# Hash attention and a two-layer block on one core: loads of three batches issued by GpSimd, and two copies moved within the second product

## The chip, the core and the metric

The kernel runs on one core of a Trainium2 chip. The core has a matrix engine (TensorE, PE), a vector engine (VectorE, DVE), an activation engine (ScalarE, ACT), a general engine (GpSimd, POOL) and a queue processor (SyncE, SP). SP, ACT and POOL can each issue DMA transfers; all of them are carried out by the core's 16 DMA engines. The metric is the device time of one execution in microseconds (us), as the median of several runs.

## The reference

```
q_bits = (q @ proj > 0); k_bits = (k @ proj > 0)          # 6 bits a row
mask   = bucket(q_bits) == bucket(k_bits)
attn   = softmax(where(mask, q @ k.T / 8, -1e9))          # rows
x      = (attn @ v) laid out as [batch, seq, heads*64]
out    = x + relu(layernorm(x) * g_ln @ w_ch1) @ w_ch2
```

There are 4 batches of 8 heads, 768 rows and 64 columns a head; the block's width is 512 and its hidden width 2048. All inputs and outputs are float32.

## The kernel before

**Chunks and rounds.** The output is made in 12 chunks of 256 rows, three to a batch. The loop over `n` (lines 867 to 882) is called a round here. In round n the kernel weaves together four things by program order: the attention of chunk n (scores L435, exponentials L445 on ACT, products with the values L469, division L489 to L497 on DVE), the norm of chunk n-1 (L516 to L518 and the transposing DMA L538 that makes `xnT`), the first product of the block for chunk n-1 ("up", L566, eight parts `u`), and the second product for chunk n-2 ("down", L607, eight parts `d`, four for each half of the chunk's rows). The last part of each half is followed by L612 on DVE, which adds the result to `x`, and by L616 on SP, which writes `x` out. The order is written out by hand in the strings of `steps`: `n` is the norm, `d` and `u` are parts of the products, and a capital with two digits is a step of the preparation of a batch and a half (four heads): `N30` is step N for batch 3, half 0. `interleave` (L681) lays these strings between the pieces of the attention by their costs.

**Preparation of a batch.** It runs a few rounds ahead, in halves. `L` loads queries and keys (`load_half`, L138), `W` loads values (`load_values`, L157). `N` makes bf16 copies on POOL (L282), `T` transposes them into `slots` by DMA (L304, then a move L309), `B` transposes 32 by 32 blocks on DVE (L287), `H` takes the hash products on PE (L318), turns them into bits on DVE (L326, L329), writes the bits to memory (L331) and reads them back in four pieces into `slots` (L333). `V` makes bf16 values and their sums on POOL (L344 to L353). `E` ("share") is one matmul of those sums on PE (L358) and a copy of its result by DVE into `vsum` (L359). `Q` squares queries and keys in place on ACT (L180), only for a check of their size; it is spread over the pairs of attention pieces by `singly`, and the load that stands beside it there follows its last step, after the eighth of a round's twelve pieces.

**Buffers.** `qnat` and `knat` have four buffers, so the load of batch b, half h, takes the buffers of batch b-2, half h, and waits until their squares are done. `vnat` has one buffer: `W` waits for the cast L344 of the values before it. The PSUM pool `ps_mm` has two banks, which the halves of the second product, the parts of the first, the hashes and the shares take by turns. A tile takes the bank that was given back first in program order. `xnT` has one buffer.

**Queues.** Each engine works its own instructions off strictly in program order, and a DMA-issuing instruction that waits holds up everything behind it on that engine. Before the change SP issues the loads of batches 2 and 3 in four pieces for each half (two heads each of q and k), the value loads of batch 1 half 1 and of batches 2 and 3, all transposing DMAs, the hash bits' eight small moves of each batch, and all outputs but the last two small ones. POOL issues the weights and the loads of batch 1 but its second value half.

The string of round 5, for instance, is

```python
5: "n d d d E20 V21 d d d d d u u u W30 u u E21 u u u",
```

and the loads beside the squares are

```python
singly = {
    2: "Q00 L20", 3: "Q01 L21", 4: "Q10 L30", 5: "Q11 L31",
    6: "Q20", 7: "Q21", 8: "Q30", 9: "Q31",
}
```

Of the kernel before, what the change touches and what calls it, by code (L numbers as in the profile page):

```python
# [30 lines left out]
def kernel(  # L31
# [11 lines left out]
    nc = tc.nc  # L43
# [83 lines left out]
    def load_half(b, half):  # L127

        h0 = half * H // 2
        t = {}  # L130
        for nm in "qk":
            t[nm] = nat.tile([P, H // 2, NC, D], F32, tag=f"{nm}nat", name=f"{nm}nat")

        cuts = [[0, 1, 2, 4] if half == 0 else [0, 2, 4], [0, 4], [0, 2, 4], [0, 2, 4]][b]
        for lo, hi in zip(cuts, cuts[1:]):
            for nm, src in (("q", q), ("k", k)):
                eng = nc.gpsimd if b == 1 else nc.scalar if nm == "k" and hi - lo == 1 else nc.sync
                eng.dma_start(  # L138
                    out=t[nm][:, lo:hi],
                    in_=src[b, h0 + lo : h0 + hi].rearrange("h (p c) d -> p h c d", p=P),  # L140
                )
        if b == 0 and half == 0:
            nc.scalar.activation(wake2[:, 0:1], wake2[:, 1:2], AF.Exp)
            t["v"] = load_values(b, half)
        return t

    def load_values(b, half):
        h0 = half * H // 2
        eng = nc.gpsimd if (b, half) == (1, 0) else nc.sync
        if (b, half) == (0, 1):  # L150

            t = work.tile([P, NH * CT // 2], F32, tag="h", bufs=1, name="vnat1")[
                :, 0 : H // 2 * NC * D
            ].rearrange("p (h c d) -> p h c d", h=H // 2, c=NC)
        else:
            t = nat.tile([P, H // 2, NC, D], F32, tag="vnat", bufs=1, name="vnat")
        eng.dma_start(  # L157
            out=t, in_=v[b, h0 : h0 + H // 2].rearrange("h (p c) d -> p h c d", p=P)
        )
        return t  # L160

    class Prep:
# [7 lines left out]
        def load(self, half):  # L170
            self.tiles.setdefault(half, {}).update(load_half(self.b, half))

        def load_v(self, half):
            self.tiles.setdefault(half, {})["v"] = load_values(self.b, half)
# [561 lines left out]
    def first_two():  # L736
# [77 lines left out]

    steps = {
# [8 lines left out]
    }  # L824
    plain = "n d d d d d d d d u u u u u u u u"
# [249 lines left out]
```

## Time and profile before

| what | value |
|---|---|
| time, median of 3 runs | 325.58 us (323.94 to 326.59) |
| time of the profiled execution | 322.48 us, of which its span is 319.8 us |
| mean granted clock of PE in it | 0.991 |
| loads issued by POOL, q and k of batch 1 | 768 KB each; median from issue to landing 14.4 us (q), 15.7 us (k) |
| the one value load issued by POOL | 17.4 us to landing |
| `xnT` transposing DMA (L538) | 10 of them, median 3.1 us to landing |
| queue q1 (issued by SP and ACT: L138, L304, L309, L331, L333, L538, L616 and others) | 31.59 MB |
| queue q0 (issued by POOL) | 8.13 MB |

The span is the time from the first instruction to the last in one profiled execution; 2.7 us of that execution's time lie outside it. "Busy" counts an engine's instructions. An idle stretch is put down to what came last before the next instruction could start; an idle stretch of an engine that is not the bottleneck costs nothing. The time to landing counts from the issue, so it holds what stood before the transfer in its queue.

### The profile page before, as it was taken

The page shows a single profiled execution, that of the slowest core. Times are in us where ns is not written, and L with a number is a line of the kernel's source. Part 1 is how long each engine was busy: PE and PEld are TensorE (multiplying, and loading weights), DVE is VectorE, ACT ScalarE, POOL GpSimd, SP SyncE. Part 2 cuts the span into 40 slices and gives each one's busy share as a digit, 9 for nine tenths or more (in the row PEclk, how much of TensorE's full clock was granted, in tenths as well). Part 3 has the DMA queues.
Part 4 walks back from the last instruction along what each step waited for, and adds up shares of the span by engine and source line. Part 5 has one row for each costly group of instructions (what it writes and reads, how often), then busy time and mean ns, then how long its engine had stood idle before and what let it go on. Part 6 is the DMA issues. An engine that isn't in the chain of part 4 may idle for free.

```text
span 319.8 us, 7815 instructions
## 1 busy us (share of the span) xinstructions
PE 304.4 (95%) x3245; PEld 228.8 (72%) x3268; DVE 187.5 (59%) x404; ACT 215.9 (68%) x272; POOL 84.8 (27%) x110
## 2 busy tenths in 40 slices
PE   7879999999999999979999999999999999999993
PEld 6556787688579669648768758769779678687563
DVE  1799996374873865723666677545643734735421
ACT  4686977776668767657777767788779667565020
POOL 3467530901900181132091091010100100100200
PEclk9999999999999999998999999999999999999998
DMA  7999997379486696492564464120030120200302
GB/s 227 363 200 301 210 340 113 66 143 255 140 166 193 162 159 148 120 338 65 183 141 103 123 143 103 29 69 34 2 87 14 28 73 1 68 35 0 101 0 76
DMA packets 64970, 40.94 MB, mean 128 GB/s; under 512 B 47152, under 2 KB 59952, under 8 KB 64928
## 3 DMA queue, kind: packets, MB, share of 16 engines
q1 hardware_dynamic: 60224, 31.59, 38.6%
q0 software_dynamic: 4128, 8.13, 10.9%
q10 hardware_dynamic: 576, 0.66, 0.6%
q8 instruction: 27, 0.44, 0.6%
q14 instruction: 15, 0.12, 0.1%
HBM read 27.98 MB, written 6.88 MB: 109 GB/s over the span
## 4 chain that ended last, share of the span: by engine, by line
PE 81%; DVE 9%; DMA 6%; issue 1%; ACT 1%; POOL 0%; SPq 0%; DVEq 0%; POOLq 0%
PE hp L566 27%; PE o L607 20%; PE sc L435 17%; PE av L469 10%; DMA xnT<-xn 5%; PE hash L318 3%; DVE slots L238 3%; DVE slots L262 2%; PE tpose L200 1%; PE o L589 1%; DMA knat<-in_k_dram 1%; DVE xn L518 1%; DVE stats L516 1%; DVE x L497 1%; PE hash L252 1%
## 5 line engine op out<-in xcount | busy, mean ns | idle before, releaser
L445 ACT ACTIVATE ex<-sc,expb 128x1024 bf16<-128x1024 f32 x144 | 159.4, 1112 | 65.7 <-PE sc L435 63.3
L566 PE MATMUL hp<-xnT,w_sb 128*128 128x256 bf16 x768 | 99.7, 274 | 3.5 <-DMA xnT<-xn 3.2
L607 PE MATMUL o<-w_sb,hbuf 128*128 128x512 bf16 x345 | 90.7, 379 | 1.8 <-DVE x L612 0.9
L435 PE MATMUL sc<-slots 70*128 70x256 bf16 x576 | 87.1, 273 | 2.3 <-POOL slots L238 1.6
L566 PEld LDWEIGHTS <-w_sb 128*128 128x128 bf16 x768 | 72.3, 98 | 13.4 <-DMA xnT<-xn 4.0
L469 PEld LDWEIGHTS <-ex 128*128 128x128 bf16 x1152 | 54.5, 98 | 15.1 <-ACT ex L445 1.3
L435 PEld LDWEIGHTS <-slots 70*128 70x128 bf16 x576 | 51.8, 97 | 18.2 <-issue 4.9
L576 DVE TENSOR_SCALAR hbuf<-hp 128x512 bf16<-128x512 f32 x48 | 32.9, 686 | 46.4 <-PE hp L566 46.3
L469 PE MATMUL av<-vaug,ex 128*128 128x65 bf16 x1152 | 59.0, 194 | 0.3 <-ACT ex L445 0.2
L529 POOL TENSOR_SCALAR rs<-mv 128x2 f32<-128x2 f32 x12 | 8.6, 713 | 168.9 <-DVE mv L517 168.8
L607 PEld LDWEIGHTS <-hbuf 128*128 128x128 bf16 x368 | 33.8, 97 | 26.9 <-issue 1.2
L612 DVE SCALAR_TENSOR_TENSOR x<-o,rs,x 128x512 f32<-128x512 f32 x23 | 17.3, 751 | 41.0 <-PE o L607 36.1
L578 ACT ACTIVATE hbuf<-hp 128x512 bf16<-128x512 f32 x48 | 28.5, 594 | 18.8 <-PE hp L566 18.8
L497 DVE TENSOR_TENSOR x<-x,rc 128x256 f32<-128x256 f32 x36 | 18.2, 506 | 1.2
L518 DVE SCALAR_TENSOR_TENSOR xn<-x,mv,gbc 128x512 bf16<-128x512 f32 x24 | 18.1, 759 | 0.8
L344 POOL CAST vaug<-vnat 128x1536 bf16<-128x1536 f32 x8 | 12.2, 1527 | 21.2 <-DMA vnat<-in_v_dram 21.2
L516 DVE BATCH_NORM_STATS2 stats<-x 128x6 f32<-128x512 f32 x24 | 16.5, 691 | 0.4
L490 DVE TENSOR_TENSOR x<-av,vsum 128x256 f32<-128x256 f32 x36 | 14.9, 414 | 0.0
L489 DVE TENSOR_SCALAR rc<-av 128x4 f32<-128x4 f32 x36 | 5.6, 157 | 13.5 <-PE av L469 13.5
L180 ACT ACTIVATE qnat<-qnat 128x768 f32<-128x768 f32 x16 | 13.3, 833 | 0.0
L180 ACT ACTIVATE knat<-knat 128x768 f32<-128x768 f32 x16 | 13.3, 833 | 0.0
L353 POOL TENSOR_TENSOR vsum<-vsum,vaug 128x256 f32<-128x256 f32 x18 | 12.5, 697 | 1.4
(86 smaller groups left out, 218.2 us busy)
## 6 DMA issues: line engine op xcount, KB each, us to landing
out_dram<-x SPq DMA_DIRECT2D x23, 256.0 KB, 4.3
vnat<-in_v_dram SPq DMA_DIRECT2D x7, 768.0 KB
qnat<-in_q_dram SPq DMA_DIRECT2D x11, 384.0 KB, 4.3
knat<-in_k_dram SPq DMA_DIRECT2D x11, 384.0 KB, 6.7
w_sb<-in_moe_w_ch_dram POOLq DMA_DIRECT2D x4, 1024.0 KB, 14.0
slots<-slots SPq DMA_DIRECT2D x6, 384.0 KB, 4.9
qnat<-in_q_dram POOLq DMA_DIRECT2D x2, 768.0 KB, 14.4
knat<-in_k_dram POOLq DMA_DIRECT2D x2, 768.0 KB, 15.7
```

Of the source, the lines that this page charges most:

```text
L180: nc.scalar.activation(src, src, AF.Square, accum_out=sq[:, a, col : col + 1],)
L435: nc.tensor.matmul(sc[:, i, :], key_block(h, kj), query_blocks(h),)
L445: nc.scalar.activation(ex, sc, AF.Exp, bias=expb[:, 1:2] if b else expb[:, 0:1], scale=scale if b else scale / Q_SCALE,)
L469: nc.tensor.matmul(av[:, h - ha, qi, :], state[g][:, i, qi * P : (qi + 1) * P], va[:, h, kj, :], start=(b > 0 and (g, i, qi) == (0, 0, 0)) ...
L497: nc.vector.tensor_tensor(xv, num, rc.unsqueeze(3).to_broadcast([P, 2, TT, D]), op=AOP.mult)
L516: nc.vector.bn_stats(stats, x[:, i, :])
L518: nc.vector.scalar_tensor_tensor(xn[:, :, i, :], x[:, i, :].rearrange("p (o d) -> p o d", d=P), mv[:, i, 0:1], gbc.rearrange("p (o d) -> p ...
L566: nc.tensor.matmul(hp[:, i, :], w1_sb[:, dt, nt * P : (nt + 1) * P], st["xnT"][:, dt, :], start=(dt == 0), stop=(dt == ND - 1),)
L576: nc.vector.tensor_scalar_max(dst, src, 0.0)
L578: nc.scalar.activation(dst, src, AF.Relu)
L607: nc.tensor.matmul(o2, st["h"][:, nt, i * P : (i + 1) * P], w2_sb[:, nt, :], start=(nt == 0), stop=(nt == NH - 1),)
L612: nc.vector.scalar_tensor_tensor(x[:, i, :], o2, st["rs"][:, i : i + 1], x[:, i, :], op0=AOP.mult, op1=AOP.add,)
```

## The change

Two things are changed. First, every load of queries, keys and values of batches 1 to 3 is now issued by POOL, and the queries and keys of a half come in one transfer of four heads each in place of two of two heads. In all 21 issues leave SP (16 of 384 KB and 5 of 768 KB) and 13 of 768 KB are added on POOL, at the same places of the program. Second, in `steps` the shares E11, E20, E30 and E31 stand two or three parts of the second product later, after its sixth part; V21 moves with E20.

```diff
-        cuts = [[0, 1, 2, 4] if half == 0 else [0, 2, 4], [0, 4], [0, 2, 4], [0, 2, 4]][b]
+        cuts = ([0, 1, 2, 4] if half == 0 else [0, 2, 4]) if b == 0 else [0, 4]
         for lo, hi in zip(cuts, cuts[1:]):
             for nm, src in (("q", q), ("k", k)):
-                eng = nc.gpsimd if b == 1 else nc.scalar if nm == "k" and hi - lo == 1 else nc.sync
+                eng = nc.gpsimd if b else nc.scalar if nm == "k" and hi - lo == 1 else nc.sync
...
     def load_values(b, half):
         h0 = half * H // 2
-        eng = nc.gpsimd if (b, half) == (1, 0) else nc.sync
+        eng = nc.gpsimd if b else nc.sync
...
-        3: "n d d d N20 d N20 B20 E11 d T20 d B20 W20 d d B20 u B20 u H20 u u u u u u",
+        3: "n d d d N20 d N20 B20 d T20 d E11 B20 W20 d d B20 u B20 u H20 u u u u u u",
...
-        5: "n d d d E20 V21 d d d d d u u u W30 u u E21 u u u",
+        5: "n d d d d d d E20 V21 d d u u u W30 u u E21 u u u",
...
-        7: "n d d d N31 d N31 B31 E30 d T31 d B31 d d B31 u B31 V31 u H31 u u u u u u",
-        8: "n d d d E31 d d d d d u u u u u u u u",
+        7: "n d d d N31 d N31 B31 d T31 d E30 B31 d d B31 u B31 V31 u H31 u u u u u u",
+        8: "n d d d d d d E31 d d u u u u u u u u",
```

On PE the order is otherwise the same but for one pair: in round 8 a group of scores and a part of the second product change places. On DVE the copies L359 of E20 and E31 move behind the L612 of the first half and the next division; those of E11 and E30 keep their place. On SP nothing changes but that the loads are gone.

## The prediction

> **What bounds the kernel now.** I read the page's shares by engine first, then the slices, then the windows and timelines around the slice that stands out.
>
> ```profile
> PE 304.4 (95%) x3245; PEld 228.8 (72%) x3268; DVE 187.5 (59%) x404; ACT 215.9 (68%) x272; POOL 84.8 (27%) x110
> PE   7879999999999999979999999999999999999993
> PEclk9999999999999999998999999999999999999998
> PE 81%; DVE 9%; DMA 6%; issue 1%; ACT 1%; POOL 0%; SPq 0%; DVEq 0%; POOLq 0%
> ```
>
> PE carries the time: 95% busy, 81% of the chain. Behind the opening (the first four slices, which the change does not touch) only the 18th of the 40 slices, 136 to 144 us, falls below nine tenths, and the granted clock dips in the 19th. In windows of 2 us (columns: length, then busy time of PE, PEld, DVE, ACT, POOL with counts; then clock, DMA share, GB/s):
>
> ```profile
> 136.00:138.00 2.00, 2.00 (x14) 1.12 (x13) 0.00 (x0) 2.00 (x4) 0.00 (x0) 1.00 1.04 371
> 138.00:140.00 2.00, 1.91 (x25) 1.25 (x23) 0.30 (x1) 1.83 (x3) 0.00 (x0) 1.00 1.03 357
> 140.00:142.00 2.00, 0.00 (x0) 0.00 (x0) 1.36 (x5) 0.83 (x3) 0.69 (x1) 1.00 1.26 237
> 142.00:144.00 2.00, 1.74 (x19) 1.56 (x20) 0.59 (x1) 0.05 (x1) 1.84 (x3) 0.87 1.00 372
> 144.00:146.00 2.00, 2.00 (x15) 1.46 (x13) 0.10 (x1) 1.07 (x1) 1.76 (x4) 0.50 0.00 0
> 146.00:148.00 2.00, 2.00 (x22) 1.67 (x20) 0.15 (x1) 1.64 (x3) 0.41 (x1) 0.77 0.00 0
> ```
>
> PE stands still while the DMA engines are full, then runs at half clock. Two rows of PE's timeline name the waits, this one and a short one a round earlier, and SP's timeline gives the cause:
>
> ```profile
> 115.20 1.05 PE L566 MATMUL hp<-xnT,w_sb 128*128 128x256 bf16 x8 [0.59 <-DMA xnT<-xn]
> 142.26 1.05 PE L566 MATMUL hp<-xnT,w_sb 128*128 128x256 bf16 x8 [2.35 <-DMA xnT<-xn]
> ```
> ```profile
> 124.53 1.59 SPq L331 DMA_DIRECT2D bits_d<-bits  x1
> 128.58 3.06 SPq L333 DMA_DIRECT2D slots<-bits_d  x4
> 131.74 0.44 SPq L138 DMA_DIRECT2D qnat<-in_q_dram  x1
> ...
> 134.81 0.41 SPq L157 DMA_DIRECT2D vnat<-in_v_dram  x1
> 135.33 2.44 SPq L538 DMA_TRANSPOSE xnT<-xn  x1
> ```
>
> SP is in order. The loads L30 stand behind the hash bits' round trip (L331 issued at 124.53, landed at 128.58, four L333), so they start at 131.74, just ahead of `xnT`; with W21 they are 2.36 MB in the same queue. `xn` was ready at 133.17 (DVE's last L518 starts at 132.42 and takes 0.75); its transpose is issued at 135.33 and lands at 142.2, 6.9 us later where the median is 3.1. In round 4 the same happens with L21: issued 106.27 to 107.86, `xnT` issued at 108.88 and landed at 115.2.
>
> **Part 1: the loads on POOL.** A load now starts when POOL reaches it and its buffer is free, whatever SP is doing.
> - L30 needs the last square of Q10, which ends at 122.45 (L180 at 121.62, 0.83). POOL's work ahead of it, V20, ends at 120.90, and POOL then sat idle 11.57 us until 132.47. So L30 goes out at 122.5 and W21 at about 124, against 131.7 and 134.8. At the 357 to 371 GB/s of the windows above, 2.36 MB take 6.5 us: landed by about 132, if bits and output share the engines by 133. SP has nothing left between the last L333 (ends 131.64) and `xnT`, which goes out at 133.2 and lands at 136.3. PE wanted it at 139.91 (142.26 less 2.35). The wait goes: **2.35 us**, with 3.6 us to spare. Next late there is nothing that the rows show: ACT waits for PE's scores on both sides of the stall (0.85 and 0.17 us), PE hardly for ACT.
> - The half clock behind it goes too. Clock lost in the last three windows: 0.13 x 2 + 0.50 x 2 + 0.23 x 2 = **1.7 us**. The Trainium skill ("TensorE: Matmul & The Clock Gate", Part 1, What's actually happening) puts the drop behind at least one idle window of about 3.4 us; here 2.35 us were enough, and the row decides. By that rule the stall would be worth its 2.35 us alone and the sum 3.8.
> - L21: Q01's last square ends at 97.5 (L180 at 96.68, 0.83); POOL is idle from 88.55 to 107.53. Issued at 97.6 in place of 106.27, its 1.57 MB land by about 104; `xnT` at 108.88 lands at 112.0, before PE's 114.61. **0.59 us** go.
> - W11, L20, W20, L31, W30, W31 move ahead or stay; no PE wait hangs on them before. W11 goes out at 64.7 (V10 ends at 64.6) against 71.08, V11 and its wait of 13.99 us move up.
> - New on POOL: 13 issues of 0.76 us (the rows of batch 1's loads: 756 to 767 ns) = 9.9 us, on an engine that waited 168.8 us for `mv`. Zero, covered by that; uncovered, at most 9.9. Each load with a wait holds back what follows on POOL: L20 (Q00 done at 70.9) holds V11, which ends about 78.5 and feeds the share at about 88; L21 holds round 4's `rs`, 10 us later and used a round on; L30 holds W21 and `rs` at 132.5; L31 (squares done at 148.8, earlier by what PE gains) holds W30 and `rs` at 159. All have room.
> - New meetings on the DMA engines: W11 with T11 and W20 with T20, each 0.79 MB, 2.2 us at the windows' rate; T20 has three rounds, T11 over 10 us. Zero. Between none and all of a load's time an `xnT` could be held; I take none, since the loads are done.
>
> **Part 2: the shares.** `ps_mm` gives out its two banks in the order of their release. With the share between the halves (E11 in round 3, E30 in round 7) it takes the second bank, and the second half must wait for the first half's L612:
>
> ```profile
> PE o L607 <- DVE x L612: 0.9, 2, 0.6
> ```
> ```profile
> 185.11 0.27 PE L358 MATMUL share<-vs,epsk 128*128 128x256 bf16 x1
> 185.93 1.02 PE L607 MATMUL o<-w_sb,hbuf 128*128 128x512 bf16 x3 [0.55 <-DVE x L612]
> ```
>
> The two waits are 0.33 us (round 3) and 0.55. Behind the sixth part the share takes the bank that L612 has long released; its copy L359 (0.41 us) gives it back while two more parts run (0.86 us each in the chain), and `u` gets it. The second half's own L612 then releases the other bank for the second `u`, as in rounds that have no share. **0.88 us** go. E20 and E31, in the middle of the first half, cost PE nothing before and nothing after. If cover fails, a wait of one L612 (0.75) comes back in each of four rounds: 3.0 us, the upper bound. V21 follows `rs` on POOL as before; its last sum now waits for E20's matmul, about 137, by when V21, started at about 134, is not done.
>
> Sum: 2.35 + 1.7 + 0.59 + 0.88 = 5.5 us. The profiled execution would go from 322.48 to 317.0. The three runs shown lie above it, their median by 3.1; carried over, 325.58 - 5.5 = **320.1**.
>
> **Rivals.**
> - *The loads still meet `xnT`.* Sixteen engines serve both queues. Batch 1's loads from POOL took 14.4, 15.7 and 17.4 us to land. At 17.4, L30 from 122.5 and W21 from 124 end at 140 to 141.5, L21 from 97.6 at 115, and `xnT` would come as late as before: only part 2's 0.88 is gained, 324.7. Against it: those loads were issued behind 4 MB of weights (1024 KB x4, 14.0 us each), and nothing is ahead of these. Chance 0.18. The Trainium skill ("DMA: Bandwidth & Descriptors", Issuing engines are not separate DMA queues) speaks for this rival: transfers from all issuers run on the same engines and interleave, and a second issuer saves only issue time; no row of before has these loads beside `xnT` in two queues, so no trace here decides it.
> - *The half clock is not in the usual run.* Then the sum is 2.35 + 0.59 + 0.88 = 3.8: 321.8. The unprofiled runs are slower than the profiled one, not faster, which speaks against. Chance 0.14.
> - *POOL's issues hold DVE, and the kernel is slower.* Beside the issues at 17.26 to 18.77 a DVE cast of 64x512 took 1.68 us (in the chain, L238 at 17.49); beside the issue at 31.74 one took 0.41. Were every one of the 13 issues a hold on a DVE step that PE waits for, 9.9 us come in and 5.5 go: 330.0. It gets slower than before from 5.5 us of holds on, by over 1% from 8.8. Against: that form of cast is not run after the opening, and DVE waits for PE 46 us at L576 alone. With the Trainium skill ("SBUF — State Buffer", SBUF: two separate sides) the two share a port by exclusive lock; no run here has these issues beside the later DVE work. Chance 0.10, for all that ends slower by over 1%.
>
> **How the numbers follow.** About 1%, 3.3 us, is what a measurement of this kernel can tell from no change. The full sum has 0.58 (320.1), without the clock 0.14 (321.8): both faster by over 1%, together 0.72. The loads that meet `xnT` (324.7) are the 0.18 within 1%; slower has 0.10. The range runs from 317.0, the full gain on the profiled execution's base, to 324.8, just over the rival that gains 0.88; it leaves out the slower cases and tails.
>
> **What would show it.** Right: L30's POOL issue near 122 less what came off ahead of it, `xnT` landing in about 3 us in rounds 4 and 5, no PE wait on it there, the 19th clock digit a 9, no wait of L607 for L612, q0 at 8.13 + 13 x 0.79 = 18.4 MB and q1 at 21.4. Wrong: `xnT` still 6 us to landing, with q0 busy beside it; a first `u` that waits for L612; DVE rows longer beside POOL's issues; a new PE wait for `vsum`, `vs` or `qnat` on POOL's side.

## The result, and the profile after

| kernel | median | runs |
|---|---|---|
| before | 325.83 us | 4, 323.94 to 326.59 |
| after | 336.02 us | 4, 333.83 to 336.61 |

The ratio is 1.0293 with a 95% interval of 1.022 to 1.0366: the change makes the kernel slower by about 3%. The profiled execution of after took 333.83 us, of which 332.1 us are its span (before: 322.48 and 319.8). Ratios and intervals, here and below, use the fast runs of each kernel alone (for after two more than the table has, 332.04 and 336.02 us), so a ratio can differ from that of two medians.

From the page of after: the shares by engine, the slices of PE and of its clock, and the chain by engine.

```profile
PE 303.9 (92%) x3245; PEld 228.0 (69%) x3268; DVE 184.9 (56%) x404; ACT 215.8 (65%) x272; POOL 94.5 (28%) x123
PE   7989999997905999999999999999999999999992
PEclk9999999999975899999999999999999999999997
PE 69%; DMA 12%; DVE 10%; POOL 3%; SPq 2%; issue 2%; ACT 1%; POOLq 0%
```

The gap that stood in the 18th slice is gone, and a larger one stands in the 12th and 13th (91 to 108 us), where the profile of before showed nothing; the clock dips in the 12th to 14th slice. PE's share of the chain fell from 81% to 69%, that of DMA rose from 6% to 12%. The windows of that stretch (length; busy time of PE, PEld, DVE, ACT, POOL with counts; clock, DMA share, GB/s):

```profile
90.00:92.00 2.00, 1.08 (x11) 0.35 (x7) 0.00 (x0) 0.48 (x1) 2.00 (x2) 1.00 0.46 102
92.00:94.00 2.00, 0.00 (x0) 0.00 (x0) 0.00 (x0) 0.00 (x0) 1.78 (x3) 1.00 0.78 190
96.00:98.00 2.00, 0.00 (x0) 0.00 (x0) 2.00 (x4) 0.00 (x0) 0.00 (x0) 0.51 0.95 328
102.00:104.00 2.00, 0.97 (x4) 0.36 (x4) 0.00 (x0) 0.94 (x1) 0.00 (x0) 0.50 1.02 199
```

From 91 to 102 us PE and ACT do next to nothing, and when PE starts again its clock is half. PE's timeline has the waits, in brackets:

```profile
83.30 1.04 PE L607 MATMUL o<-w_sb,hbuf 128*128 128x512 bf16 x4 [2.48 <-issue]
...
101.93 1.04 PE L435 MATMUL sc<-slots 70*128 70x256 bf16 x4 [10.85 <-DMA slots<-bits_d]
104.28 1.89 PE L566 MATMUL hp<-xnT,w_sb 128*128 128x256 bf16 x8 [1.32 <-DMA xnT<-xn]
```

SP's and POOL's timelines have the cause:

```profile
63.63 10.92 SPq L304 DMA_TRANSPOSE slots<-nat  x1
89.29 0.70 SPq L309 DMA_DIRECT2D slots<-slots  x1
90.03 0.93 SPq L616 DMA_DIRECT2D out_dram<-x  x1
91.07 1.59 SPq L331 DMA_DIRECT2D bits_d<-bits  x1
95.19 5.83 SPq L333 DMA_DIRECT2D slots<-bits_d  x4
101.12 1.28 SPq L538 DMA_TRANSPOSE xnT<-xn  x1
```
```profile
63.57 0.83 POOL L157 DMA_DIRECT2D vnat<-in_v_dram  x1
64.40 0.75 POOL L138 DMA_DIRECT2D qnat<-in_q_dram  x1
70.26 0.75 POOL L138 DMA_DIRECT2D knat<-in_k_dram  x1 [5.11 <-ACT knat L180]
80.04 1.67 POOL L344 CAST vaug<-vnat 128x1536 bf16<-128x1536 f32 x1 [9.03 <-DMA vnat<-in_v_dram]
```

POOL issues W11 and L20's q in the same microsecond in which SP issues T11, the transposing DMA of batch 1's second half. The move L309 waits for T11 and is issued at 89.29: T11 took 25.7 us (before 5.7: 64.56 to 70.30). Its landing is read from L309 here and below. SP is in order, so the bits' round trip, an output and `xnT` all stood behind it: PE waits 10.85 us for bits that it needs for the scores, and DVE 8.07 us for that output before it may write `x` again. W11 itself landed after 16.4 us, so V11 started at 80.04 (before 78.59). The chain of waits says the same in one piece:

```profile
63.63 25.65 DMA slots<-nat
```

By the issues of `xnT`, from T11 to round 3's the time grew from 22.21 to 37.49 us (+15.28), and to round 4's by 1.14 more (the clock is half at first). From round 4 to round 8 it fell from 100.31 to 95.47 us: the forecast gain is there, 4.84 us, with no wait for `xnT` in rounds 4 and 5. With T11 0.93 earlier, the last `xnT` is 15.28 + 1.14 - 4.84 - 0.93 = 10.65 us late; another 1.6 us of the span come after PE's last matmul.

### The profile page after: what moved, and what is told of

Its sections match the earlier page's. It is cut to its first block, busy times and chain, and to the rows that moved or that the text cites. A ratio compares the mean times of both kernels' runs of the same rounds, so it can differ in the third digit from the quotient of the medians.

```text
span 332.1 us, 7794 instructions
## 1 busy us (share of the span) xinstructions
PE 303.9 (92%) x3245; PEld 228.0 (69%) x3268; DVE 184.9 (56%) x404; ACT 215.8 (65%) x272; POOL 94.5 (28%) x123
## 3 DMA queue, kind: packets, MB, share of 16 engines
q1 hardware_dynamic: 53232, 21.36, 30.8%
q0 software_dynamic: 6624, 18.35, 21.9%
## 4 chain that ended last, share of the span: by engine, by line
PE 69%; DMA 12%; DVE 10%; POOL 3%; SPq 2%; issue 2%; ACT 1%; POOLq 0%
PE hp L566 23%; PE o L607 17%; PE sc L435 15%; PE av L469 8%; DMA slots<-nat 8%; DVE slots L238 2%; DMA xnT<-xn 2%; PE hash L318 2%; SPq L333 2%; DVE slots L262 2%; DMA bits_d<-bits 1%; DVE stats L516 1%; DVE xn L518 1%; PE o L589 1%; PE tpose L200 1%
## 5 line engine op out<-in xcount | busy, mean ns | idle before, releaser
L607 PE MATMUL o<-w_sb,hbuf 128*128 128x512 bf16 x345 | 90.0, 379 | 3.2 <-issue 2.5
L607 PEld LDWEIGHTS <-hbuf 128*128 128x128 bf16 x368 | 33.6, 97 | 28.2 <-issue 2.8
L612 DVE SCALAR_TENSOR_TENSOR x<-o,rs,x 128x512 f32<-128x512 f32 x23 | 17.2, 749 | 41.0 <-PE o L607 34.3
L497 DVE TENSOR_TENSOR x<-x,rc 128x256 f32<-128x256 f32 x36 | 15.7, 436 | 1.2
L138 POOL DMA_DIRECT2D knat<-in_k_dram x6 | 4.5, 757 | 34.6 <-ACT knat L180 34.6
```

The costliest lines, as they stand in the source:

```text
L497: nc.vector.tensor_tensor(xv, num, rc.unsqueeze(3).to_broadcast([P, 2, TT, D]), op=AOP.mult)
L607: nc.tensor.matmul(o2, st["h"][:, nt, i * P : (i + 1) * P], w2_sb[:, nt, :], start=(nt == 0), stop=(nt == NH - 1),)
L612: nc.vector.scalar_tensor_tensor(x[:, i, :], o2, st["rs"][:, i : i + 1], x[:, i, :], op0=AOP.mult, op1=AOP.add,)
```

## The experiments

W11 and L20 are the loads beside T11 in round 2; W20 and L21 are those beside T20 and round 3's `xnT`. "The sum" is what the transfers take alone, one behind the other.

**1. Parts of the change** (four kernels on one chip; before there 325.69, 320.42 to 327.16).

The first: the new `steps`, all loads as before.

> The kernel before with the four shares moved and no load moved. Both theories agree here: the two waits of L607 for L612 (0.33 and 0.55 us) go, nothing else moves. Expected 0.9 us less than before, about 324.9 against 325.8; no such wait in the profile, the wait for xnT in round 5 still there.

Measured 322.97 us (320.5 to 325.54), ratio 1.0011 (0.9924 to 1.0098): no change that can be told, in an interval wider than the 0.9 us looked for. No wait of L607 for L612 is left, but in its profiled execution, the longest of the six (325.54), round 5's `xnT` cost PE 4.39 us (2.35 before).

The second puts W11 and L20 back on SP (this diff and the next are against the changed kernel):

```diff
-        eng = nc.gpsimd if b else nc.sync
+        eng = nc.sync if (b, half) == (1, 1) or not b else nc.gpsimd
-                eng = nc.gpsimd if b else nc.scalar if nm == "k" and hi - lo == 1 else nc.sync
+                eng = nc.sync if (b, half) == (2, 0) else nc.gpsimd if b else nc.scalar if nm == "k" and hi - lo == 1 else nc.sync
```

> The changed kernel with two of its load steps, W11 and L20, given back to SP behind T11; the other ten POOL loads stay. Theory A (the loss is T11's transposing DMA run beside loads of another queue): T11 lands in about 6 us, no PE wait for slots in round 3, and the gain of rounds 4 and 5 is all that is left: about 320.5. Theory B (POOL's issuing itself costs, by holding DVE or by slow descriptors): 8 of the 11 new transfers stay, so most of the loss stays: over 330.

Measured 323.22 (318.34 to 324.03), ratio 0.9947 (0.9737 to 1.0157). T11 is back at 5.6 us (64.77 to 70.38) and the large gap is gone. (Of the 13 new transfers ten stay on POOL, as the first sentence of the expectation has it; its "8 of the 11" is a slip.) In the profiled execution, the longest of the four (324.03), a wait comes one round later: W20 (87.99) and q of L21 (88.83) now run beside `xnT`, issued at 87.68.

```profile
94.33 1.89 PE L566 MATMUL hp<-xnT,w_sb 128*128 128x256 bf16 x8 [4.97 <-DMA xnT<-xn]
```

The third and fourth keep one of the two on POOL: W11 (only the second edit), then L20 (only the first).

> The changed kernel with L20 on SP; W11 alone stays on POOL beside T11. Theory A, with a cost in proportion to the load's packets (T11's 25.7 us less 5.7 alone, over three transfers of 768 KB: 6.7 us each): T11 lands in about 12.4 us, which round 3's scores can bear, so about 320.5. Theory A without proportion (one load that starts with T11 is enough): T11 over 20 us and about 334. If only bytes shared the engines: T11 5.7 + 2.2 = 7.9 us.

> The changed kernel with W11 on SP behind T11; L20's q starts on POOL about 1 us after T11, its k about 6 us later. Theory A in proportion: T11 lands in about 5.7 + 2 x 6.7 = 19 us, the scores of round 3 wait some 2 to 4 us, about 323 to 326. Without proportion: T11 over 20 us and over 330. If only bytes shared the engines: T11 about 10 us and 320.5.

With W11 alone 333.69 (328.1 to 334.61), ratio 1.0254 (1.0033 to 1.0475). One load of 768 KB was enough; SP's timeline of that run:

```profile
64.45 10.48 SPq L304 DMA_TRANSPOSE slots<-nat  x1
80.57 0.70 SPq L309 DMA_DIRECT2D slots<-slots  x1
```

T11 took 16.1 us. PE waited 7.03 us for the bits and 6.55 for `xnT`. With L20 alone 336.82 (335.07 to 342.22), ratio 1.0431 (1.0326 to 1.0535): T11 took 13.1 us, then T20, issued at 94.97 beside W20 and L21, 21 us (L309 at 116.03); round 4's `xnT` came 11.49 us late for PE. Each load alone leaves the kernel slow, by other waits: in the fourth run most of it is T20's meeting.

How much of this is more than sharing? From the times alone (5.7 us for T11 in before, 4.2 to 4.9 for a load, measured in experiment 3) estimates of the sums follow. T11 with W11: 9.9 to 10.6, measured 16.1. T11 with all three loads of after: 18.3 to 20.4, measured 25.7. T11 with L20's two loads: 14.1 to 15.5, measured 13.1. T20 (5.5 alone, in the gated kernel of experiment 2) with W20 and L21: 18.1 to 20.2, measured 21. So by this estimate most of what T11 lost in after, 12.6 to 14.7 of 20 us, is the time of three loads; 5 to 7 us go beyond the sum. None of the expected times of T11 (7.9, 12.4 or over 20 with W11; 10, 19 or over 20 with L20) came.

**2. Apart in time, same queue** (this kernel, the sixth and the first of experiment 3 on one chip; before 324.88, 321.43 to 328.1). All 13 loads stay on POOL, but before W11 and W20 POOL reads two elements of what T11 or T20 writes, so these loads start once the transposing DMA has landed:

```diff
+    gate = consts.tile([P, 2], BF16, name="gate")
...
+            if (self.b, half) in ((1, 1), (2, 0)):
+                nc.gpsimd.tensor_copy(gate, self.pair_places(half)[:, 0, 0, 0:2])
             self.tiles.setdefault(half, {})["v"] = load_values(self.b, half)
```

> The changed kernel with nothing given back to SP: all 13 issues stay on POOL, but ahead of W11 and of W20 POOL reads one pair of elements of what T11 and T20 write, so W11, L20, W20 and L21 start only when the transpose before them has landed. Theory A' (a load that starts in another queue beside a transposing DMA slows both, wherever that happens): T11, T20 and every xnT land in under 7 us, no PE wait over 1 us from round 3 on, 5.5 us or more under before: 317 to 320.5 where before has about 325.7. Rival B (POOL's issuing or its queue as such): all 13 issues are still there, over 330. Rival C (it is only the bytes that share 16 engines): the same bytes at nearly the same time, the loss mostly stays.

Measured **317.41 us** (316.67 to 322.63, 6 runs), ratio **0.9788 (0.9741 to 0.9835)**: faster than both kernels. POOL's timeline and two lines of the page:

```profile
70.34 0.18 POOL L177 COPY gate<-slots 128x2 bf16<-128x2 bf16 x1 [5.56 <-DMA slots<-nat]
70.58 0.83 POOL L159 DMA_DIRECT2D vnat<-in_v_dram  x1
71.41 0.75 POOL L140 DMA_DIRECT2D qnat<-in_q_dram  x1
72.15 0.75 POOL L140 DMA_DIRECT2D knat<-in_k_dram  x1
```
```profile
PE   7879999999999999999999999999999999999991
PEclk9999999999999999999999999999999999999998
```

T11 (64.70 to 70.30) and T20 (88.74 to 94.23) take 5.6 and 5.5 us again. W11 waits 5.56 us for it, which nobody notices. Neither a gap nor half clock is left behind the opening, but for the last slice. This shows that the loss came from loads that ran beside T11 and T20; it does not tell plain sharing from what goes beyond it, since both end when the loads wait.

The sixth kernel moves W11, L20, W20 and L21 to SP and leaves the rest on POOL, without any gate:

```diff
-        eng = nc.gpsimd if b else nc.sync
+        eng = nc.sync if (b, half) in ((1, 1), (2, 0)) or not b else nc.gpsimd
-                eng = nc.gpsimd if b else nc.scalar if nm == "k" and hi - lo == 1 else nc.sync
+                eng = nc.sync if (b, half) in ((2, 0), (2, 1)) else nc.gpsimd if b else nc.scalar if nm == "k" and hi - lo == 1 else nc.sync
```

> The changed kernel with W11, L20, W20 and L21 on SP, the rest on POOL. Theory A': as with the gate, but L21 stands again ahead of round 4's xnT on SP, so the 0.6 us or so of that wait stays: 318 to 321. Rival B: 7 of 13 issues stay, about half the loss, 330.

Measured 319.65 (318.67 to 323.68, 10 runs), ratio 0.9854 (0.9814 to 0.9894). The gain comes with the later loads on POOL alone; the gated kernel is ahead because on SP the early ones still delay `xnT`:

```profile
90.93 1.05 PE L566 MATMUL hp<-xnT,w_sb 128*128 128x256 bf16 x8 [2.01 <-DMA xnT<-xn]
115.57 1.05 PE L566 MATMUL hp<-xnT,w_sb 128*128 128x256 bf16 x8 [0.48 <-DMA xnT<-xn]
```

**3. The pair by itself.** Four kernels that only run transfers of the kernel's sizes and shapes, in stages, to price the meeting.

> A kernel that computes nothing of the reference: after zeros are written to the output it runs twelve stages three times over, each waiting for the one before: the 786 KB transpose alone, the 768 KB load alone (POOL, SP), a plain copy of 786 KB, and pairs of them. Theory A': transpose beside a POOL load over 12 us, where alone it is about 6 and the load about 3.5; a plain copy beside the same load no longer than the sum, about 6. Whether ACT's queue does the same decides between 'a second queue' (over 12) and 'GpSimd's descriptors' (about 8). Transpose and load both on SP: the sum, about 8. Load issued well ahead of the transpose: the sum. Rival C: every pair takes the sum of its parts.

Alone, the transposing DMA takes 5.4 us, POOL's load 4.2 to 4.9, SP's 4.6, an ordinary copy 5.15. POOL's load with the transposing DMA took 8.4 to 9.5 us together, ACT's 7.3 to 7.5. So two transfers hardly overlap, but they never cost more than their sum, and 16.1 us was not reproduced.

> Again a kernel that computes nothing of the reference (zeros go to the output): nine stages three times over. In the stages before, the POOL load's first packet came 4 us after its issue, when the 5.4 us transpose was almost done, so the two hardly met. Here the transpose is issued after the load by a filler on VectorE of one, two or three parts, so that they do meet; also beside a load on ACT's queue, beside VectorE's own 32x32 transposes, and with a plain copy in the transpose's place. Theory A' (they slow each other where they meet): one of the POOL stages takes over 14 us from the load's issue, where a sum of the parts is about 10 to 12. Theory D (GpSimd's descriptors are held up by VectorE's work, and the transpose behind them): only the stages with VectorE's work are slow, the load alone with it too. If no stage exceeds the sum, neither is shown, and what makes T11 slow is something else in round 2.

With delays and with block transposes on DVE beside them: 7 to 9.5 us, again within the sum.

> A third kernel apart from the reference (zeros to the output). In the stages so far one of the two was always nearly through before the other's first packet ran. Here the transpose is issued from about 0 to 1.5 us after the POOL load in steps of some 0.25 us, also behind a 256 KB output store in its own queue as in round 2, beside a load on ACT's queue, and with a plain copy in its place; each stage twice. Theory A' (they hold each other up where both are under way): some stages take over 14 us until both have landed, with few packets of either in the microseconds between, and none of the plain copies does. Rival E (the pair alone is harmless at any offset, and round 2 has another partner): every stage stays within the sum, 9 to 10 us from the load's issue.

Every offset from 0 to 1.5 us gave 7.3 to 8.7 us. But the offset of the issues is not the order of the packets. The traces record each packet: the transposing DMA has 3072 of 256 bytes. In all the isolated kernels the first packet of POOL's load ran when at most 227 of them, or at least 2835, had landed. In the changed kernel it ran after 756 and with W11 alone after 583, the two cases well beyond the sum; for T11 with L20 alone, within the sum, it ran before the first. So the meeting that is slow in the kernel was not reproduced in isolation.

> By itself: this kernel leaves out the reference's computation and writes zeros. Ten stages, run through twice; the first has GpSimd's load of 768 KB and SP's transposing DMA of 768 KB alone, the next six the same pair beside one kind of work of the other engines: 44 matmuls of 512 columns on PE; nine exponentials of 1024 columns on ACT; ten block transposes of 768 columns on DVE; twelve float32 sums on DVE; twenty-four casts on DVE; exponentials, matmuls and block transposes together. Then the transposing DMA alone beside the three together, the load alone beside them, and a load from ACT's queue with the transposing DMA beside them. Theory F: the pair is slow in the kernel (16.1 us for T11 beside one load) because the engines are at work; then one of the stages with work beside it takes over 12 us where the pair alone takes about 8, and the stage names the engine. If the transposing DMA alone beside the work takes as long, the load has no part in it. Rival E: nothing of the engines' work bears on it; all stages with the pair take 7 to 9.5 us, the transposing DMA alone 5.4, the load alone 4.2 to 4.9, and what makes the pair slow in the kernel is another thing, left open.

The seven stages with the pair ended 8.1 to 9.6 us after the load's issue in the first pass, whatever worked beside them; the longest had casts on DVE. Theory F is not borne out, in the order of packets that these stages had.

**4. Another queue, and the shares** (one chip; before 325.24, 321.93 to 327.0). In the gated kernel W11 and L20 are issued by ACT without a gate, and the gate before W20 stays:

```diff
-        eng = nc.gpsimd if b else nc.sync
+        eng = nc.scalar if (b, half) == (1, 1) else nc.gpsimd if b else nc.sync
-                eng = nc.gpsimd if b else nc.scalar if nm == "k" and hi - lo == 1 else nc.sync
+                eng = nc.scalar if (b, half) == (2, 0) else nc.gpsimd if b else nc.scalar if nm == "k" and hi - lo == 1 else nc.sync
-            if (self.b, half) in ((1, 1), (2, 0)):
+            if (self.b, half) == (2, 0):
```

> The changed kernel with W11 and L20 issued by ACT in its own hardware queue (W20 and L21 behind the gate on POOL, as in the gated kernel, so that only round 2 differs from it). Theory A' for any second queue: T11 again takes over 12 us and the time is 325 or more. If it is a matter of GpSimd's queue alone: T11 lands in 8 to 10 us and the time is that of the gated kernel, 317 to 320.

Measured 319.4 (317.46 to 322.11), ratio 0.9853 (0.9724 to 0.9982). T11 took 15.9 us (64.60 to 80.49) beside all three loads, against 25.7 beside the same loads from POOL; PE waits 2.66 us for round 3's `xnT`. Loads of ACT's queue make T11 late too, but 15.9 us is less than the four transfers' sum (18.3 to 20.4 by the estimate above, with POOL's loads), and the time is the one expected if it were GpSimd's queue alone. More than the sum was seen beside POOL's loads only: ACT's first packet ran after 495 of T11's, and in isolation after 453 to 488, and both stayed within it.

The gated kernel with the old `steps`:

> The gated kernel with the shares where they were before. Both theories: the two waits of L607 for L612 come back, 0.9 us more than the gated kernel, about 318.3 against 317.4.

Measured 317.55 (317.21 to 319.09), ratio 0.9813 (0.9718 to 0.9908), 0.14 us from the gated kernel with the new ones. The wait of 0.55 us for L612 is back in its profile, and one of 0.78 for `vs`, yet the time does not show them; the runs spread over more than the 0.9 us in question.

**5. What in the meeting costs so much** (one run each; before 328.01). In the kernel with W11 alone beside T11, first T11 as an ordinary copy, then W11 split in two, 384 KB by POOL and the rest by SP behind T11:

```diff
-            nc.sync.dma_start_transpose(
-                out=self.pair_places(half)[:, :, 0, :],
-                in_=self.nat16[half].rearrange("p h a c d -> p (h a c d)"),
-            )
+            if (self.b, half) == (1, 1):
+                nc.sync.dma_start(
+                    out=self.pair_places(half)[:, :, 0, :],
+                    in_=self.nat16[half].rearrange("p h a (i two) d -> p (h a i) (two d)", two=2),
+                )
+            else:
+                nc.sync.dma_start_transpose(
+                    out=self.pair_places(half)[:, :, 0, :],
+                    in_=self.nat16[half].rearrange("p h a c d -> p (h a c d)"),
+                )
```
```diff
+        if (b, half) == (1, 1):
+            nc.gpsimd.dma_start(
+                out=t[:, 2:4], in_=v[b, h0 + 2 : h0 + 4].rearrange("h (p c) d -> p h c d", p=P)
+            )
+            nc.sync.dma_start(
+                out=t[:, 0:2], in_=v[b, h0 : h0 + 2].rearrange("h (p c) d -> p h c d", p=P)
+            )
+            return t
```

> The kernel with L20 on SP (W11 alone beside T11), but T11 an ordinary copy of the same 768 KB to the same places instead of a transposing DMA: the operands of batch 1, half 1 are not transposed, so the transposition of that half is left out. Theory G: it is the transposing DMA that suffers inside the kernel when another queue's packets come between its own: then the ordinary copy and W11 are both done within about 10 us (5.2 and 4.2 alone) and PE's wait for the bits of round 3 is gone. Rival H: any SBUF-to-SBUF transfer suffers there: the copy takes 13 us or more, like T11's 16.1.

> The same kernel, with W11 cut: heads 2 and 3 (384 KB) by GpSimd beside T11, heads 0 and 1 by SP behind T11. If the excess over the sum of the two transfers goes with the amount that interleaves, T11 takes about half the excess: 5.7 + 2.1 alone = 7.8, plus 3, about 11 us. If any load in the other queue beside it is enough, it stays at 14 to 16 us. If it is a threshold or chance, T11 takes 8 us or less.

SP's timeline of the first, where the copy is L305 and the move behind it L315:

```profile
64.14 0.68 SPq L305 DMA_DIRECT2D slots<-nat  x1
74.30 0.65 SPq L315 DMA_DIRECT2D slots<-slots  x1
```

The ordinary copy took 10.2 us, about the sum (5.15 + 4.2 to 4.9), and PE's wait for the bits shrank to 0.51 us, as theory G has it. The time, 327.35, stayed high because round 3's `xnT`, also transposing, met W20 and L21 and cost PE 7.86 us. With half of W11 the transposing DMA took 8.2 us, close to the sum of 7.8 and near neither the 11 nor the 14 to 16 us of the first two cases; the time was 324.31.

Neither run settles its question, for in both the order of the packets changed as well. POOL issued W11 0.44 us ahead of the copy and 0.70 us ahead of T11 (with W11 whole and T11 transposing: 0.05), and its first packet ran before the other's first. When nine tenths of the load's packets had landed, only 245 of the copy's 3072 and 212 of T11's had. T11 with L20 alone, a transposing DMA beside whole loads, had that order too and stayed within its sum. So the kind of the DMA and the amount are both open.

What stays open: why the pair exceeds its sum inside the kernel (16.1 against about 10) and not by itself. That a load of POOL's queue must cut in while the transposing DMA has a fifth to a quarter of its packets done is a lead from the packet records, not shown: no run set that order on purpose, and the kernel's own mixture of smaller transfers was not tried either.

## Why the prediction was wrong

**The step that failed** is the last of part 1, "New meetings on the DMA engines: W11 with T11 and W20 with T20, each 0.79 MB, 2.2 us at the windows' rate; T20 has three rounds, T11 over 10 us. Zero." It found the pair, and got price and room wrong. The price took a rate of 357 to 371 GB/s from windows full of loads. A load by itself takes 4.2 to 4.9 us, not 2.2, and T11 alone fills the engines at less, about 200 GB/s in the gated kernel (first two rows). Beside the loads, the two slowest windows of after show full engines that move a ninth of the rate (last two rows):

```profile
66.00:68.00 2.00, 2.00 (x29) 1.80 (x26) 1.97 (x4) 2.00 (x4) 0.00 (x0) 1.00 1.09 211
68.00:70.00 2.00, 2.00 (x25) 1.79 (x24) 2.00 (x4) 1.34 (x3) 0.00 (x0) 1.00 0.99 188
...
66.00:68.00 2.00, 2.00 (x27) 1.80 (x25) 2.00 (x4) 1.34 (x2) 0.00 (x0) 1.00 1.83 42
68.00:70.00 2.00, 2.00 (x27) 1.81 (x25) 2.00 (x4) 2.00 (x5) 0.00 (x0) 1.00 0.95 41
```

T11 lasted 20 us longer, not 2.2: by the estimate of experiment 1, 12.6 to 14.7 for the time of three loads, the rest beyond any sum and unexplained. The gated kernel shows that the loss lay in the meetings: same issuer, same 13 transfers, W11 and W20 with what follows them held apart from T11 and T20, 317.41 us. The room of "over 10 us" was T11's own; the queue behind it (L309, an output, the bits) was not followed to PE. Nor were T20's three rounds room: in the fourth run of experiment 1 round 4's `xnT` stood behind it and PE waited 11.49 us.

**L20's partner was missed too.** The step names W11 with T11. L20's q followed it 0.83 us later, k at 70.26, in the same meeting, and L21's q is issued directly behind W20 (93.03, and not after both of Q01's squares, as "issued at 97.6" had it), so where T11 was not late (the second experiment) it meets `xnT` and T20. The term covered an `xnT` held for at most one load's time; here whole queues stood behind several loads.

**Right: the gain in rounds 4 and 5.** 4.84 us came off from round 4 to round 8, where the sum's terms without round 3's 0.33 give 5.2: the two waits, the half clock, and at most 0.55 of the shares. No wait for `xnT` in rounds 4 and 5, full clock there, q0 with 18.35 MB and q1 with 21.36 came as forecast.

**The shares' 0.88** went out of the waits, but moved the time by nothing that could be told, in the kernel of before (1.0011) and in the gated one (0.14 us). A gain of that size would be lost in these intervals, so its size is open.

**The rivals.** *The loads still meet `xnT`* had the right mechanism, contention across queues, but in the wrong round and upon another transfer: it looked at rounds 4 and 5, where nothing meets. The Trainium skill ("DMA: Bandwidth & Descriptors", Issuing engines are not separate DMA queues) has transfers of all issuers on the same engines; the isolated pair agrees (8.4 to 9.5 us for 5.4 and 4.2 to 4.9 alone). The pair in the kernel (16.1) took more than such sharing gives. *POOL's issues hold DVE* is not what made it slower: the gated kernel has all 13 issues and no such loss. *The half clock is not usual* is not borne out: the six executions of the gated kernel have a clock of 0.988 to 0.998, five of them 0.996 or more; the 17 of before on that chip have 0.980 to 0.995. But a stall of that length does not always bring it: in the kernel with ACT's loads PE waited 2.66 us and no slice of its clock is below nine tenths (mean 0.998), so "2.35 us were enough" holds for that stall and is no rule.

**The forecast itself.** With the meeting taken out, 324.88 - 317.41 = 7.5 us were to be had against before on that chip (6.9 by the ratio), more than the 5.5 of the sum. The profiled executions are nearer to it: 322.48 before, 317.43 gated, where the sum had 317.0. The stalls of the other runs of before were likely longer, as the 4.39 us in the first experiment suggests, but that is argued, not shown.

## What to carry to other kernels

A load moved to a second issuer no longer stands behind that queue's transfers; it runs beside them. List, for each load moved, what the old order kept it behind, and price the meeting by at least the sum of what the transfers take alone, and by everything that waits behind them in their queues, not by bytes over a rate. Where the old order was a useful one, keep it with a wait: here two tiny reads of 0.18 us each turned a loss of 3% into a gain of 2%.

## What was not expected of the hardware

- A transposing DMA of 768 KB that takes 5.4 to 5.7 us alone took 16.1 us beside one load of 768 KB from POOL, where the sum of the two is about 10, and 25.7 beside three from POOL, where the sum is 18.3 to 20.4. Beside three from ACT it took 15.9, less than the sum.
- In the run with 16.1 us the DMA engines were full and moved 60 and 68 GB/s in the windows from 68 to 72 us (share 1.17 and 0.97).
- By itself the same pair took 7.3 to 9.6 us at every offset and beside every kind of work tried, with the load's packets ahead of nearly all of the other's or behind nearly all of them.
- PE's wait of 2.48 us "for issue" in after (80.8 to 83.3) follows on a packet of the instruction queue that lasted 3.1 us by the packet records (78.8 to 81.9; 0.9 to 1.7 us elsewhere in before and after). That instructions come late when the DMA engines are held is a guess from that; it wasn't tried.
